# A decode block's last eight attention rounds in another order, products that fill TensorE's waits at the end, and another first inverse root

## The chip, the cores and the metric

The kernel runs on one core of one Trainium2 chip. A core has TensorE (PE, the matrix engine, with its weight loads shown as PEld), VectorE (DVE), ScalarE (ACT), GpSimd (POOL), SyncE (SP, which only issues transfers here) and 16 DMA engines. Each engine runs its own instructions strictly in the order in which the kernel wrote them, and waits on semaphores for the others. The metric is device time in microseconds (us) of one execution; lower is better.

## The reference

One decode step of a small transformer block in fp32: batch 4, model width 512, 32 query heads over 8 key/value heads, 4096 cached positions, head width 128, then a token-mixing MLP of width 1792.

```python
mod = (silu(c) @ w_mod).reshape(4, 6, 1, -1)          # sa, ca, ga, sb, cb, gb
h = layernorm(x) * (1 + ca) + sa
q = h @ wq
scores = q . k_cache * 128 ** -0.5                    # per batch and kv head
o = softmax(scores) @ v_cache
x = x + ga * (o @ wo)
h = layernorm(x) * (1 + cb) + sb
hn = layernorm(h)                                     # inside the mixer
u = gelu(hn * w1 + b1)                                # (batch, 512 channels, 1792)
x = x + gb * (u @ w2 + b2)
```

The caches are 128 MiB, the other weights some 22 MiB; nearly all of the work is to read them once.

## The kernel before

There are 32 rounds, one for each pair of batch (4) and key/value head (8); round i has a key tile K(i) and a value tile V(i) of 2 MiB each. A ring of three buffers of 4 MiB takes them: a load brings K(i+2) and V(i) together (line 192); near the end the loads come in smaller parts (lines 213 and 220), and the value tile of round 31 in four (32 position groups, cut at 16, 24 and 28). A load into a buffer waits until TensorE has used what was in it. All loads are issued by SP on one queue.

The steps of round i, as the table of the last eight rounds names them:

- `s` scores on TensorE (line 240), `S` row maximum on VectorE (245), `m` turn it (249), `X` maximum over the four column groups (254), `b` spread it to all partitions (260), `B` copy it (265), `e` exponential on ScalarE with a row sum (270).
- `t` transposes the two halves of the exponentials on VectorE (277); `l` sums over groups on TensorE (281), `L` their reciprocal and a selection matrix on VectorE (286, 292; in round 31 286, 289).
- `v` the product with the values on TensorE (303; in round 31 line 311, in four parts), `V` its copy out of PSUM (317), `a` picks and scales the heads (326), `A` copies (331), `p` multiplies by the output weights (339; in rounds 30 and 31 line 344, into one common accumulator `pgx`), `P` adds to the running sum of the batch (353, 355).

After a batch's eight rounds the mixer for it follows: fold (`F`, 360), residual and statistics (`R`, 364 to 374), two layer norms (`G`, `M`, `H`, `Q`, `N`), seven times an expansion `x` on VectorE (439, two of the 14 columns of w1 each), `g` gelu on ScalarE (495) and `c` the contraction with w2 on TensorE (444). Batches 0 to 2 run their mixers beside the next batch's rounds; batch 3's mixer comes at the end, after everything else. `f` (575) multiplies an eighth of the last two heads' output weights by the gate ga, so that rounds 30 and 31 need no gate at the end; `y` (360) folds rounds 24 to 29, `E` (364, 365) makes gate and residual of it, and `I` (693) adds that into `pgx` on TensorE.

For rounds 0 to 23 a loop writes the steps in a fixed order. For the last eight rounds the table `PLAN` is the order, written out by hand: the kernel walks through its words, and each word writes one step, so the table sets the order of instructions on every engine at once. `manual_schedule` leaves that order alone. `LP`, `LK`, `LV`, `LW` are loads and `LT` takes the next ring buffer; `T`, `T2`, `T3` load ScalarE's function tables early by a dummy call.

Batch 3's tail, the words from `zs` on, is a serial chain: statistics of `pgx` (`zs`), gather (`zq`, `zg`), the inverse root and the modulation (`zm`, `adaln_last`), spreading (`zb`), the second gather and norm (`zn`, `affine`), and `finish`: the 14 columns' gelus in seven groups, each followed by its contraction on TensorE, then the output. In `adaln_last` ScalarE makes a first value of the inverse root (407) and VectorE refines it by one step (409, 410) beside the difference from the mean (408); line 411 puts both together.

Of the kernel before, what the change touches and what calls it, by code (L numbers as in the profile page):

```python
# [8 lines left out]
F32 = mybir.dt.float32  # L9
I32 = mybir.dt.int32  # L10
AF = mybir.ActivationFunctionType
OP = mybir.AluOpType
# [21 lines left out]
def adaln_decode(ctx: ExitStack, tc: tile.TileContext, small, x, wmod, wq, kk, kv, vv, wo, out):  # L34
# [365 lines left out]

    def adaln_last(b, pst):
        mean, var = norm(pst)
        y = wk.tile([P, 1], F32, name="ye")
        t = wk.tile([P, 1], F32, name="te")
        a = wk.tile([P, P], F32, name="a")
        h1 = wk.tile([P, P], F32, name="h1")
        nc.scalar.activation(y, var, AF.Abs_reciprocal_sqrt, scale=1.0 / C2)
        dv.scalar_tensor_tensor(a, XK[:, b], mean, prep[:, 3], op0=OP.subtract, op1=OP.mult)
        dv.scalar_tensor_tensor(t, y, var, y, op0=OP.mult, op1=OP.mult)
        dv.scalar_tensor_tensor(y, t, 3.0 * C2, y, op0=OP.subtract, op1=OP.mult)  # L410
        dv.scalar_tensor_tensor(h1, a, y, prep[:, 2], op0=OP.mult, op1=OP.subtract)
        return h1, stats(h1, b)

    def bcast(h1, b, pb=None, cs=range(4)):
# [4 lines left out]
            mm(pb[:, c, :], ident[:, e:e + 1].to_broadcast([P, P]), h1, start=True, stop=True)  # L419
        return pb.rearrange("p c n -> p (c n)")  # L420

    def affine(pst, pb, times):
# [4 lines left out]
        if times is w1:  # L427
# [3 lines left out]
        if times is w1:  # L431
            nc.gpsimd.tensor_tensor(wr, w1, y.to_broadcast([P, NF]), op=OP.mult)
        else:
            rsqrt(var, P, "e", out=wr, times=times)
        return hb, wr

    def expand(u, hb, wr, js):
# [15 lines left out]
    class Mixer:  # L453
# [25 lines left out]
            self.pb = bcast(self.h1, self.b, pb, cs)  # L479

        def normalise(self):
            self.hb, self.wr = affine(self.st, self.pb, w1n if self.b < B - 1 else w1)
            self.py = None

        def expand(self, u=None):
# [53 lines left out]

    def finish(b, pg, py, hb, wr):  # L540
        uu = ring.tile([P, 16, D], F32, name="uu", tag="kv")
        for js in ((0,), (1,), (2, 3, 4), (5, 6, 7), (8, 9, 10), (11, 12), (13,)):
            j = js[0]
            if j < 2:
                nc.scalar.activation(uu[:, j], hb, AF.Gelu_apprx_tanh, bias=b1[:, j:j + 1], scale=wr[:, j:j + 1])
                u = uu[:, j:j + 1]
            else:
                u = uu[:, j:j + len(js)]
                expand(u, hb, wr, js)
                nc.scalar.activation(u, u, AF.Gelu_apprx_tanh)  # L550
# [8 lines left out]
        dv.scalar_tensor_tensor(osb[:, b], py, b2, gbl, op0=OP.add, op1=OP.mult)  # L559
        dv.tensor_add(osb[:, b], osb[:, b], XK[:, b])  # L560
        nc.sync.dma_start(dst[b], osb[8 * b:P:32, b])
# [75 lines left out]
    x LP27 m26 S27 f P24 m27 X26 X27 f b26 B26 e26 x b27 v25.1 c g t26.1 l25 t26.0 B27 s28 V25 c g L25  # L637
    v26.0 v26.1 S28 x l26 f a25 L26 V26 A25 x m28 p25 LT X28 e27 c a26 P25 t27.0 A26 b28 s29 f B28 p26 e28
    LK30 t27.1 S29 P26 v27.0 m29 l27 g LK31 T t28.1 X29 LT t28.0 s30 L27 S30 b29 v27.1 B29 e29 l28 m30 V27
    c LV28 L28 a27 g X30 t29.1 t29.0 l29 L29 s31 A27 LV29 b30 p27 x v28.0 B30 S31 m31 e30 f P27 LT LV30 X31  # L640
    v28.1 b31 l30 B31 e31 LV31 V28 L30 c t30.1 a28 l31 L31 v29.0 t31.1 v29.1 A28 p28 t30.0 V29 a29 v30.0
    A29 LW f v30.1 P28 p29 g V30 t31.0 a30 x v31.0 v31.1 v31.2 P29 A30 Y y f v31.3 p30 E V31 a31 I A31 p31
    zs g zq zg T2 c zx c zm zq zb0 zc T3 zg zb1 zw0 zn zw1
# [8 lines left out]
    for step in PLAN.split():  # L652
# [90 lines left out]
```

## Time and profile before

Each time is of one execution. The page's chain of waits is followed back from the last instruction; the lists of instructions in order of time give start and duration in us, engine, line, operation, written tile, read tiles, shapes, count, and in brackets how long the engine had been idle and whose work ended that.

| what | value |
|---|---|
| time, three runs | 389.9, 389.29, 389.33 us, median 389.33 |
| time of the profiled execution | 389.85 us |
| its span, first to last instruction | 387.7 us |
| mean clock granted to TensorE | 0.890 of full |
| moved by DMA | 157.70 MB, mean 407 GB/s |
| busy: PE, DVE, ACT | 297.5, 213.9, 107.9 us (77, 55, 28% of the span) |

Busy shares are means over the whole span. What counts for a change at the end is which wait ends last there.

### The profile page before, as it was taken

The numbers are of one execution on the slowest core, as the hardware profiler recorded it, in microseconds if no ns is written. First come the engines' busy times: TensorE is split into PE (matmuls) and PEld (weight loads), VectorE is DVE, ScalarE is ACT, GpSimd is POOL, SyncE is SP. The second block draws the span as 40 slices with busy tenths as digits, with TensorE's granted clock in tenths as the row PEclk, the third lists the DMA queues.
The fourth block names the chain that finished last, engine by engine and source line by source line (L and its number), as shares of the span: only waits on it lengthen the run. The fifth ranks groups of instructions, "written<-read, shape, count | busy, mean of one in ns | idle before, by whom it ended". The sixth has DMA issues, their size and how long they took to land.

```text
span 387.7 us, 5709 instructions
## 1 busy us (share of the span) xinstructions
PE 297.5 (77%) x2416; PEld 121.0 (31%) x2416; DVE 213.9 (55%) x510; ACT 107.9 (28%) x130; POOL 1.5 (0%) x8
## 2 busy tenths in 40 slices
PE   0776685962966829778788859999888886999984
PEld 0122121330322302234222323353323342445472
DVE  0420361530453605677666644767766678788666
ACT  0001120110110111114557110114782104657156
POOL 0000000000000000000000000000000000000000
PEclk9989666795596979999999995979999999799899
DMA  8999999999999999999999999999999999999900
GB/s 329 433 433 433 416 445 433 416 448 431 414 450 433 433 433 431 433 431 433 432 433 432 433 431 433 433 431 430 431 433 431 433 431 433 414 426 427 389 28 3
DMA packets 7281, 157.70 MB, mean 407 GB/s; under 512 B 964, under 2 KB 980, under 8 KB 1368
## 3 DMA queue, kind: packets, MB, share of 16 engines
q1 hardware_dynamic: 7248, 157.33, 94.6%
q8 instruction: 19, 0.31, 0.3%
q14 instruction: 6, 0.05, 0.0%
q10 hardware_dynamic: 8, 0.00, 0.0%
HBM read 157.32 MB, written 0.01 MB: 406 GB/s over the span
## 4 chain that ended last, share of the span: by engine, by line
DMA 43%; PE 36%; DVE 16%; ACT 3%; issue 1%; SPq 0%; ACTq 0%; DVEq 0%
DMA kv<-in_kv 41%; PE s L240 9%; PE pv L303 8%; DVE m L245 3%; PE pt L326 3%; PE pa L339 3%; DVE p L277 3%; PE s L139 2%; PE qs L154 2%; DMA sm<-in_small 2%; PE pb L260 2%; DVE mx L254 2%; ACT uu L550 1%; DVE acc L355 1%; PE py L444 1%
## 5 line engine op out<-in xcount | busy, mean ns | idle before, releaser
L240 PE MATMUL s<-kv,QT 128*32 128x512 f32 x512 | 75.4, 708 | 41.5 <-DMA kv<-in_kv 39.4
L270 ACT ACTIVATE p<-s,nm 128x1024 f32<-128x1024 f32 x32 | 35.6, 1114 | 196.2 <-DVE nm L265 196.1
L245 DVE TENSOR_REDUCE m<-s 128x1 f32<-128x1024 f32 x32 | 39.2, 1223 | 80.1 <-PE s L240 80.1
L303 PE MATMUL pv<-kv,p 128*32 128x512 f32 x496 | 75.0, 685 | 0.1
L277 DVE STREAM_TRANSPOSE p<-p 128x512 f32<-128x512 f32 x64 | 41.9, 687 | 1.7 <-ACT p L270 1.7
L240 PEld LDWEIGHTS s<-kv,QT 128*32 128x32 f32 x512 | 15.6, 121 | 85.6 <-DMA kv<-in_kv 53.9
L326 PEld LDWEIGHTS pt<-sel,po 128*128 128x128 f32 x250 | 33.1, 206 | 28.6 <-issue 17.5
L339 PE MATMUL pa<-wo,oT 128*32 128x512 f32 x240 | 35.0, 657 | 3.9 <-DVE oT L331 3.8
L326 PE MATMUL pt<-sel,po 128*128 128x4 f32 x250 | 35.7, 266 | 1.3 <-DVE po L317 1.3
L317 DVE COPY po<-pv 128x512 f32<-128x512 f32 x31 | 21.4, 689 | 17.2 <-PE pv L303 17.1
L254 DVE TENSOR_REDUCE mx<-pm 1x128 f32<-1x512 f32 x32 | 21.4, 671 | 0.7 <-PE pm L249 0.7
L495 ACT ACTIVATE u<-u 128x1024 f32<-128x1024 f32 x20 | 20.4, 1051 | 2.7 <-DVE u L439 2.6
L439 DVE TENSOR_SCALAR u<-hb,wr,sm 128x512 f32<-128x512 f32 x40 | 19.9, 540 | 1.0 <-PE py L450 0.9
L260 PEld LDWEIGHTS pb<-neg,mx 1*128 1x128 f32 x64 | 10.2, 198 | 32.6 <-DVE mx L254 30.9
L270 ACT ACT_TABLE_LOAD x11 | 14.1, 1283 | 20.5 <-DVE nm L265 20.4
L355 DVE TENSOR_TENSOR acc<-acc,pa 128x512 f32<-128x512 f32 x26 | 17.7, 681 | 2.4 <-PE pa L339 2.4
L139 PE MATMUL s<-wm,sT 128*4 128x512 f32 x16 | 9.7, 773 | 12.1 <-DVE sT L125 12.1
L303 PEld LDWEIGHTS pv<-kv,p 128*32 128x32 f32 x496 | 14.5, 147 | 8.0 <-issue 3.5
L260 PE MATMUL pb<-neg,mx 1*128 1x1 f32 x64 | 12.9, 268 | 5.0 <-DVE mx L254 5.0
L495 ACT ACT_TABLE_LOAD x13 | 16.7, 1283 | 0.2
L249 PE MATMUL pm<-ident,m 128*1 128x128 f32 x32 | 9.0, 283 | 9.7 <-DVE rl L286 4.0
L249 PEld LDWEIGHTS pm<-ident,m 128*1 128x1 f32 x32 | 2.5, 80 | 39.0 <-DVE rl L286 22.2
(146 smaller groups left out, 210.9 us busy)
## 6 DMA issues: line engine op xcount, KB each, us to landing
kv<-in_kv SPq DMA_DIRECT2D x28, 4096.0 KB, 21.3
wq<-in_wq SPq DMA_DIRECT2D x2, 4096.0 KB
wo<-in_wo SPq DMA_DIRECT2D x4, 2048.0 KB, 25.2
kv<-in_kv SPq DMA_DIRECT2D x4, 2048.0 KB, 17.6
wm<-in_wmod SPq DMA_DIRECT2D x2, 2048.0 KB, 7.9
kv<-in_kk SPq DMA_DIRECT2D x1, 4096.0 KB
kv<-in_vv SPq DMA_DIRECT2D x3, 1024.0 KB
wm<-in_wmod SPq DMA_DIRECT2D x1, 1024.0 KB
```

The costliest lines, as they stand in the source:

```text
L240: mm(s[32 * c:32 * c + 32, n * 512:(n + 1) * 512], QT[:, b, h, :], KT[i][:, (n * 4 + c) * 512:(n * 4 + c + 1) * 512], start=True, stop=True)
L245: dv.tensor_reduce(M[i], S[i], axis=AX.X, op=OP.max)
L254: dv.tensor_reduce(mx, M[i].rearrange("o (c r) -> o r c", c=4).unsqueeze(1).to_broadcast([1, 4, 32, 4]), axis=AX.X, op=OP.max)
L260: mm(pb, M[i].rearrange("o c r -> o (c r)"), neg1, start=True, stop=True)
L270: nc.scalar.activation(p, S[i], AF.Exp, bias=M.pop(i), accum_out=l)
L277: dv.transpose(p, p)
L303: mm(PV[i][32 * q:32 * q + 32, :], pT[:, 128 * k:128 * k + 128:4], VT[i][:, 4 * k:4 * k + 4, :].rearrange("p j d -> p (j d)"), start=(k < ...
L317: dv.tensor_copy(PV[i], pv)
L326: mm(pt, po[:, c * DH:(c + 1) * DH], sel[:, c, :], start=(c == 0), stop=(c == n - 1))
L339: mm(pa[32 * g:32 * g + 32, :], oT[:, g:g + 1].to_broadcast([P, 32]), wo_t[h][:, g, :], start=True, stop=True)
L355: dv.tensor_add(ACC[b], ACC[b], pa)
L495: nc.scalar.activation(u, u, AF.Gelu_apprx_tanh)
```

## The change

It has three parts.

First, the table `PLAN` is written in another order between round 23's `a` and round 31's `p`; the steps are the same, and from `zs` on the table is the same.

Second, in `finish` TensorE gets five more products after the contractions of columns 0, 1, 2 to 4, 5 to 7 and 8 to 10: the identity times 128 or 256 columns of a weight already in SBUF, into a PSUM tile `pad` that nobody reads.

Third, in `adaln_last` the inverse root is a reciprocal on VectorE and then a square root on ScalarE, with no refinement; the table that `T2` loads is the square root's. The sign of the modulated row is now the usual one, so `affine` uses the negated w1 for all batches.

```diff
     def adaln_last(b, pst):
         mean, var = norm(pst)
-        y = wk.tile([P, 1], F32, name="ye")
-        t = wk.tile([P, 1], F32, name="te")
+        q = wk.tile([P, 1], F32, name="qe")
+        r = wk.tile([P, 1], F32, name="ye")
         a = wk.tile([P, P], F32, name="a")
         h1 = wk.tile([P, P], F32, name="h1")
-        nc.scalar.activation(y, var, AF.Abs_reciprocal_sqrt, scale=1.0 / C2)
+        dv.reciprocal(q, var)
+        nc.scalar.activation(r, q, AF.Sqrt)
         dv.scalar_tensor_tensor(a, XK[:, b], mean, prep[:, 3], op0=OP.subtract, op1=OP.mult)
-        dv.scalar_tensor_tensor(t, y, var, y, op0=OP.mult, op1=OP.mult)
-        dv.scalar_tensor_tensor(y, t, 3.0 * C2, y, op0=OP.subtract, op1=OP.mult)
-        dv.scalar_tensor_tensor(h1, a, y, prep[:, 2], op0=OP.mult, op1=OP.subtract)
+        dv.scalar_tensor_tensor(h1, a, r, prep[:, 2], op0=OP.mult, op1=OP.add)
         return h1, stats(h1, b)
...
     def finish(b, pg, py, hb, wr):
         uu = ring.tile([P, 16, D], F32, name="uu", tag="kv")
+        pad = ps_e.tile([P, D], F32, name="pad", tag="e")
+        hold = {0: 128, 1: 256, 2: 256, 5: 256, 8: 256}
         for js in ((0,), (1,), (2, 3, 4), (5, 6, 7), (8, 9, 10), (11, 12), (13,)):
...
             contract(py, u, js)
+            if j in hold:
+                mm(pad[:, :hold[j]], ident, WM[5][:, 0, :hold[j]], start=True, stop=True)
...
     PLAN = """
-    a23 v24.0 A23 p23 t25.0 P23 F R v24.1 LP25 G s26 t25.1 M H V24 LP26 Q a24 S26 v25.0 N s27 x A24 f p24 g
...
+    LP25 t25.0 a23 A23 p23 P23 F v24.0 R v24.1 G s26 f M H Q t25.1 V24 LP26 a24 s27 N A24 S26 x v25.0
...
         elif step == "T2":
-            nc.scalar.activation(tab, neg1, AF.Abs_reciprocal_sqrt)
+            nc.scalar.activation(tab, ones[0:1, 0:1], AF.Sqrt)
```

What the new table does to the engines is seen in their instructions. The numbers behind the names count buffers; `x` is the two TENSOR_SCALAR that write `u`, `f` the TENSOR_TENSOR that writes `wo6`.

TensorE from round 31's scores (`s31`) to round 30's products with the values, before (`wo2` and `wo4` are output weights, `g32` and `grpl` are helpers for sums over groups):

```order
L240 MATMUL s31_2274<-kv_2146,QT_121 32x512 x8
L260 MATMUL pb_2286<-neg1_87,mx_2264 128x1
L339 MATMUL pa_2288<-wo2_126,oT_2283 32x512 x4
L303 MATMUL pv_2296<-kv_2211,p_2188 32x512 x4
L249 MATMUL pm_2305<-ident_99,m_2303 1x128
L303 MATMUL pv_2296<-kv_2211,p_2188 32x512 x4
L260 MATMUL pb_2321<-neg1_87,mx_2315 128x1
L281 MATMUL pl_2323<-l_2308,grp_117 128x1
L444 MATMUL py_2066<-u_2136,sm_88 32x128 x8
L326 MATMUL pt_2349<-sel_2256,po_2334 128x4 x4
L281 MATMUL pl_2354<-l_2328,grpl_119 128x1
L303 MATMUL pv_2360<-kv_2211,p_2236 32x512 x8
```

And of the change, at the same place:

```order
L240 MATMUL s31_2276<-kv_2080,QT_121 32x512 x8
L260 MATMUL pb_2286<-neg1_87,mx_2258 128x1
L339 MATMUL pa_2289<-wo2_126,oT_2268 32x512 x4
L303 MATMUL pv_2297<-kv_2220,p_2188 32x512 x4
L249 MATMUL pm_2306<-ident_99,m_2302 1x128
L303 MATMUL pv_2297<-kv_2220,p_2188 32x512 x4
L260 MATMUL pb_2319<-neg1_87,mx_2309 128x1
L443 MATMUL py_2047<-u_2148,sm_88 32x128 x8
L281 MATMUL pl_2339<-l_2316,grp_117 128x1
L326 MATMUL pt_2349<-sel_2255,po_2325 128x4 x4
L281 MATMUL pl_2354<-l_2343,grpl_119 128x1
L303 MATMUL pv_2361<-kv_2220,p_2238 32x512 x8
```

Only the contraction (`py`) and round 30's sum `l30` (`pl`) have changed places; from `v29` on, row by row, TensorE's order up to `finish` is the same in both kernels.

VectorE beside it, around round 31's row maximum `S31`, before:

```order
L439 TENSOR_SCALAR u_2293<-hb_1997,wr_1998,sm_88 128x512 x2
L265 COPY nm_2301<-pb_2286 128x1
L245 TENSOR_REDUCE m_2303<-s31_2274 128x1
L575 TENSOR_TENSOR wo6_128<-wo6_128,gate_1845 128x512
L355 TENSOR_TENSOR acc_2041<-acc_2041,pa_2288 128x512
L254 TENSOR_REDUCE mx_2315<-pm_2305 1x128
L265 COPY nm_2325<-pb_2321 128x1
L317 COPY po_2334<-pv_2296 128x512
```

And of the change:

```order
L438 TENSOR_SCALAR u_2294<-hb_2000,wr_2001,sm_88 128x512 x2
L245 TENSOR_REDUCE m_2302<-s31_2276 128x1
L265 COPY nm_2304<-pb_2286 128x1
L355 TENSOR_TENSOR acc_2043<-acc_2043,pa_2289 128x512
L254 TENSOR_REDUCE mx_2309<-pm_2306 1x128
L578 TENSOR_TENSOR wo6_128<-wo6_128,gate_1845 128x512
L265 COPY nm_2321<-pb_2319 128x1
L317 COPY po_2325<-pv_2297 128x512
```

`S31` now stands ahead of `B30` (the COPY that writes `nm` for round 30's exponential), and one `f` stands behind `X31` (line 254) where it stood ahead of `P27` (line 355).

VectorE from the last copy of a round's values to the modulation of the tail, before (line 317 with `pve` is `V31`):

```order
L331 COPY oT_2446<-pt_2409 128x4
L575 TENSOR_TENSOR wo6_128<-wo6_128,gate_1845 128x512
L364 TENSOR_TENSOR ep_2475<-pc_2449,prep_129 128x128
L365 TENSOR_TENSOR ep_2475<-ep_2475,prep_129 128x128
L317 COPY po_2478<-pve_2416 128x128
L331 COPY oT_2483<-pt_2480 128x4
```

And of the change:

```order
L331 COPY oT_2416<-pt_2409 128x4
L355 TENSOR_TENSOR acc_2043<-acc_2043,pa_2402 128x512
L317 COPY po_2474<-pve_2418 128x128
L364 TENSOR_TENSOR ep_2478<-pc_2449,prep_129 128x128
L365 TENSOR_TENSOR ep_2478<-ep_2478,prep_129 128x128
L331 COPY oT_2482<-pt_2476 128x4
L578 TENSOR_TENSOR wo6_128<-wo6_128,gate_1845 128x512
```

`V31` now stands ahead of `E` (lines 364, 365), and the last `f`, which was written ahead of `E`, now stands behind `A31` (the second COPY of `oT`), directly ahead of round 31's product with the output weights, whose last quarter reads what it writes.

More of the change, by code (lines that the diff above doesn't have):

```diff
@@ L420, in bcast, with affine @@
         return pb.rearrange("p c n -> p (c n)")
-    def affine(pst, pb, times):
+    def affine(pst, pb, last):
         mean, var = norm(pst)
@@ L425, in affine @@
         wr = wk.tile([P, NF], F32, name="wr")
-        if times is w1:
+        if last:
             y = wk.tile([P, 1], F32, name="ye")
@@ L430, in affine @@
         nc.scalar.activation(hb, pb, AF.Identity, bias=mean, scale=-1.0)
-        if times is w1:
-            nc.gpsimd.tensor_tensor(wr, w1, y.to_broadcast([P, NF]), op=OP.mult)
+        if last:
+            nc.gpsimd.tensor_tensor(wr, w1n, y.to_broadcast([P, NF]), op=OP.mult)
         else:
-            rsqrt(var, P, "e", out=wr, times=times)
+            rsqrt(var, P, "e", out=wr, times=w1n)
         return hb, wr
@@ L635, in adaln_decode @@
     PLAN = """
-    a23 v24.0 A23 p23 t25.0 P23 F R v24.1 LP25 G s26 t25.1 M H V24 LP26 Q a24 S26 v25.0 N s27 x A24 f p24 g
[L637 to L643, printed above, removed]
+    LP25 t25.0 a23 A23 p23 P23 F v24.0 R v24.1 G s26 f M H Q t25.1 V24 LP26 a24 s27 N A24 S26 x v25.0
+    LP27 S27 f m26 p24 X26 g x P24 m27 c f b26 X27 v25.1 B26 b27 l25 e26 x t26.0 g t26.1 LT x B27 s28
+    V25 v26.0 S28 c g l26 L25 v26.1 a25 f L26 c V26 A25 e27 x m28 p25 X28 P25 a26 t27.0 A26 b28 s29 f
+    B28 v27.0 e28 LK30 p26 t27.1 S29 P26 m29 l27 s30 X29 g LK31 T t28.1 LT t28.0 S30 b29 L27 v27.1 B29
+    V27 e29 l28 m30 c L28 LV28 X30 a27 g t29.1 t29.0 A27 l29 L29 s31 LV29 b30 LT p27 x v28.0 S31 B30 m31
+    P27 X31 v28.1 e30 f b31 B31 LV30 V28 c LV31 l30 t30.1 e31 L30 a28 l31 t31.1 L31 v29.0 v29.1 A28 LW
+    p28 t30.0 g V29 a29 v30.0 t31.0 v30.1 A29 f P28 p29 V30 a30 x A30 v31.0 v31.1 v31.2 Y P29 y v31.3
+    p30 V31 a31 E I A31 f p31 zs g zq zg T2 c zx c zm zq zb0 zc T3 zg zb1 zw0 zn zw1
     """
```

2 lines of the change are left out of this document (1 added, 1 removed).

## The prediction

> **What bounds the kernel now.** I read the page's slices first, then the transfers' issues, then TensorE in order of time from round 31 on, then the clock by stretches of the gate's own length, and last the tail.
>
> ```profile
> span 387.7 us, 5709 instructions
> PEclk9989666795596979999999995979999999799899
> DMA  8999999999999999999999999999999999999900
> ```
>
> A slice is 9.69 us. The DMA engines are full from the start to slice 38, whatever the compute engines do. Then come two slices of tail. So a step of the table matters only if it makes a transfer land later, or if it lies behind the last landing.
>
> ```profile
> 350.39 0.43 SPq L220 DMA_DIRECT2D kv<-in_vv  x1
> kv<-in_vv SPq DMA_DIRECT2D x1, 256.0 KB, 17.5
> ...
> 353.26 0.22 PEld L303 LDWEIGHTS pv<-kv,p 128*32 128x32 f32 x8 [0.73 <-DMA kv<-in_kv]
> ```
>
> The last piece of round 31's values lands at 350.39 + 17.5 = 367.9. It was issued 17 us ahead, so a release that comes several us later or earlier leaves the landing where it is. And at 353.26 TensorE had been idle for 0.73 us for round 28's values: whatever was lost or won in rounds 24 to 30 was made up there, with 0.73 us to spare.
>
> ```profile
> 354.49 1.09 PE L303 MATMUL pv<-kv,p 128*32 128x512 f32 x8
> 356.24 0.64 PE L444 MATMUL py<-u,sm 128*32 128x128 f32 x16
> 356.84 1.05 PE L326 MATMUL pt<-sel,po 128*128 128x4 f32 x8
> 357.75 0.36 PE L281 MATMUL pl<-l,grpl 128*128 128x1 f32 x2
> 358.21 3.20 PE L303 MATMUL pv<-kv,p 128*32 128x512 f32 x16
> 361.11 1.61 PE L339 MATMUL pa<-wo,oT 128*32 128x512 f32 x8
> 363.63 1.95 PE L303 MATMUL pv<-kv,p 128*32 128x512 f32 x16
> 365.40 1.04 PE L339 MATMUL pa<-wo,oT 128*32 128x512 f32 x8
> ```
>
> Round 29's values are 2048 KB behind round 28's. At the 431 GB/s of the row below (351.95) that is 2.10 MB / 431 = 4.9 us, so they land at about 353.2 + 4.9 = 358.1: `v29`, at 358.21, sits on its landing too. It took 3.20 us where `v30`, of the same shape, took 1.95, and `p28` 1.61 where `p29` took 1.04. That is 1.25 + 0.57 = 1.8 us lost to the clock:
>
> ```profile
> 351.95:355.37 3.42, 3.42 (x31) 0.96 (x27) 3.19 (x6) 2.49 (x3) 0.00 (x0) 1.00 1.01 431
> 355.37:358.78 3.41, 3.29 (x42) 2.52 (x42) 2.46 (x9) 2.48 (x3) 0.00 (x0) 1.00 0.97 411
> 358.78:362.19 3.41, 3.41 (x24) 0.88 (x16) 1.77 (x4) 1.07 (x2) 0.00 (x0) 0.50 1.01 418
> 379.26:382.67 3.41, 1.73 (x50) 1.20 (x50) 3.41 (x8) 3.41 (x4) 0.00 (x0) 1.00 0.00 0
> 382.67:386.09 3.42, 1.80 (x48) 1.12 (x48) 1.65 (x5) 1.41 (x2) 0.00 (x0) 1.00 0.03 7
> ```
>
> Columns: stretch, its length, busy us of PE, PEld, DVE, ACT, POOL, granted clock, DMA share, GB/s. The clock was halved for 3.41 us behind a stretch in which PE counts as busy for 3.29 us, but mostly with small products: four columns (356.84) or one (357.75). So the sparse stretch that costs something is the one between `v28`'s second half (354.49) and `v29`.
>
> **The change, part by part.** The sum is made against the profiled execution, 389.85 us (span 387.7 and 2.15 around it). The median of the runs, 389.33, is 0.52 lower, so I carry the difference over to the median.
>
> *Rounds 24 to 30.* The same steps stand in another order; no transfer is added and SP's order stays. A gain here ends at 353.26, since `v28` waits for its landing: 0. A loss is free up to 0.73 us and beyond that moves `v28` and `v29` one for one. A load's cover, at the last piece, is 17.5 us less the 0.6 us that 256 KB need at 431 GB/s; a release would have to come more than ten us late to leave the queue empty. I take 0.
>
> *Round 31's `S31` ahead of `B30`.* TensorE's order is the same there but for one exchange, so what decides is VectorE.
>
> ```profile
> 352.56 1.21 DVE L245 TENSOR_REDUCE m<-s 128x1 f32<-128x1024 f32 x1
> 352.72 1.28 ACT L270 ACT_TABLE_LOAD   x1 [0.97 <-DVE nm L265]
> 354.02 1.11 ACT L270 ACTIVATE p<-s,nm 128x1024 f32<-128x1024 f32 x1
> 356.28 1.11 ACT L270 ACTIVATE p<-s,nm 128x1024 f32<-128x1024 f32 x1 [1.06 <-DVE nm L265]
> ```
>
> `B30` was at 352.5 and now follows `S31`, at about 353.6. ScalarE then loads the table until 355.1, does `e30` until 356.2 and its sum until 356.3, and `e31` until about 357.5 instead of 357.4: the 1.06 us for which ScalarE waited ahead of `e31` take the delay up. `l31` (357.75) comes behind `a28`, which ends at 357.9. So `v29` moves by 0 to 0.1: +0.05. The cover is gone as soon as `S31` itself is late, which is the slower rival.
>
> *From `v29` to round 31.* TensorE's order is unchanged, and so is the sparse stretch ahead of it. I therefore keep the halved clock: 0.
>
> ```profile
> 368.43 0.68 DVE L575 TENSOR_TENSOR wo<-wo,gate 128x512 f32<-128x512 f32 x1
> 369.15 0.40 PE L311 MATMUL pve<-kv,p 128*32 128x128 f32 x8
> 369.37 1.06 PE L344 MATMUL pgx<-wo,oT 128*32 128x128 f32 x32
> 369.94 0.28 DVE L317 COPY po<-pve 128x128 f32<-128x128 f32 x1
> 370.36 0.30 PEld L326 LDWEIGHTS pt<-sel,po 128*128 128x128 f32 x2 [0.20 <-DVE po L317]
> 371.00 1.08 PE L344 MATMUL pgx<-wo,oT 128*32 128x128 f32 x32
> ```
>
> *`V31` ahead of `E`.* `V31` ran at 369.94, 0.4 us after round 31's last values (369.15 + 0.40), because `E` stood ahead. `a31` waited 0.20 us for it; now that wait goes, but `p30` holds TensorE until 370.43. Bounds 0 and -0.20; I take -0.1. `E` ends later, at about 370.5, just as `I` needs it. The last `f` (0.68 us) now starts with `p31` behind `A31`; it must be done for `p31`'s last quarter, which begins three quarters of 1.08 us = 0.81 later. Bounds 0 and +0.1, taken into the range.
>
> *The inverse root.*
>
> ```profile
> 350.89 0.12 DVE L286 RECIPROCAL rl<-pl 128x1 f32<-128x1 f32 x1
> 373.46 0.35 DVE L408 SCALAR_TENSOR_TENSOR a<-xk,mv,prep 128x128 f32<-128x128 f32 x1
> 373.46 0.20 ACT L407 ACTIVATE ye<-mv 128x1 f32<-128x1 f32 x1 [3.00 <-DVE mv L389]
> 374.18 0.35 DVE L411 SCALAR_TENSOR_TENSOR h<-a,ye,prep 128x128 f32<-128x128 f32 x1
> ```
>
> Before, 374.18 - 373.46 = 0.72 us lie between statistics and modulation. Now: reciprocal 0.12 to 0.17, then `a` 0.35 on VectorE, beside it ScalarE's square root, priced as line 407's 0.20, each with a hand-over below 0.1. That makes 0.50 to 0.55: -0.2 (bounds -0.25 and -0.1). One table is loaded in place of another; the gelu's table then loads 0.2 later, under the wait for `hb`.
>
> *The five filling products.*
>
> ```profile
> 375.38 0.69 PE L419 MATMUL py<-h,ident 128*128 128x128 f32 x4
> 382.66 1.89 PE L444 MATMUL py<-uu,sm 128*32 128x128 f32 x48 [0.51 <-ACT uu L550]
> 383.61 0.68 PEld L444 LDWEIGHTS py<-uu,sm 128*32 128x32 f32 x24 [0.35 <-ACT uu L550]
> 384.62 0.35 DVE L559 SCALAR_TENSOR_TENSOR osb<-py,sm,gbl 128x128 f32<-128x128 f32 x1 [0.92 <-PE py L444]
> ```
>
> Two products of the identity with 128 columns took 0.69 (375.38), so one of 256 takes at most that, and about 0.5 when only its columns count. The first four lie in waits for ScalarE. The fifth does not: behind columns 8 to 10 (begun 382.66) TensorE waited only 0.35 us, until 383.61. The fill pushes the last contractions by 0.15 to 0.34, and 0.1 of that is won back ahead of column 13. Bounds 0 and +0.45; I take +0.15.
>
> Sum: 0.05 - 0.1 - 0.2 + 0.15 = -0.1 us, 389.2 on the median. With the bounds of these terms alone, and half a us of wander as between the runs shown, the case spans 388.6 to 389.9.
>
> The fills are there for the clock. In the Trainium skill, "TensorE: Matmul & The Clock Gate", section "HAM oscillation — how this bites in real kernels", the rule of thumb is that no idle gap of TensorE may exceed about 3.4 us. By that rule the tail, whose waits are far shorter, keeps its clock anyway and the fills only cost: the same -0.1. The trace does not bear the rule out as it stands: the clock fell at 358.78 behind a stretch with 0.12 us idle.
>
> **The rivals.** *Faster: the clock falls differently.* The tail's stretches in rows 379.26 and 382.67 have 1.7 to 1.8 us of short products and kept the clock in this trace. The stretch from 355.37 lost it; there only `v28`'s end (0.2 us), one contraction (0.64) and `v29`'s start (0.6) stream many columns, about 1.4 us in all. So the tail is near the edge. If stretches fall 1 us later, one holds only the first columns' contractions, and the last ones run at half speed. Columns 8 to 13 took 1.89 us with their waits; at half speed the products would need up to 1.7 us more, of which the waits for ScalarE hide a part. I estimate a cost of 0.9 to 1.3 us in such runs of the kernel before, which the fills take away: 389.3 - 0.9 - 0.1 = 388.3. Or the halved clock at `v29` is missed: round 31's last products then follow their landing at 367.9 instead of 369.15, -1.25, also about 388.2. Against it: one trace, with the tail at 1.00. The Trainium skill, same page, section "What's actually happening", states that the window of 3413 ns is free-running and does not reset with the kernel; the stretches of 3.41 us agree, but only several traces could show that they shift between executions.
>
> *Slower: VectorE late at `S31`.* It was busy for 3.19 of the 3.42 us from 351.95, and the new table has other steps ahead of `S31`. If `S31` begins 1 us later than 352.5, `e30`'s table load, `e30` and `e31` follow, `l31` holds TensorE, and `v29` starts at about 359.2; with the clock halved it all arrives 0.9 later: 389.2 + 0.9 = 390.1 to 390.3. It decides from about 0.2 us of lateness on. Against it: the 0.73 us of slack at `v28`, and VectorE's work ahead of this place is the same steps.
>
> *No effect at all on the path* is within the first case, since three of its four terms are 0.2 or less.
>
> **Chances.** A measurement of this kernel can tell about 0.2%, 0.8 us, from no change. The first case, 389.2, has 0.50; the faster one (below 388.55) 0.33; the slower one (above 390.1) 0.17. The range reaches into both: 388.0 to 390.2.
>
> **What would show it.** `v28` again waits for its transfer at about 353.2 and `v29` starts at 358.2; `v29` takes about 3.2 us if the clock falls again, 1.9 if not. The wait of `a31` for `V31` is gone. From the second-last statistics to `h` there are about 0.5 us. The last contraction starts behind the fifth fill, not behind ScalarE. Wrong would be: `v28` without a wait, a gap in the DMA share before 366, or a clock of 1.00 from 355 to 366.

## The result and the profile after

The changed kernel takes 391.59 us (median of 6 runs, 390.36 to 392.05), the kernel before 389.30 in the 6 runs beside it (388.78 to 389.90): a ratio of 1.0053 with a 95% interval of 1.0033 to 1.0074. It is slower by about 2 us, where 389.2 was predicted. (A ratio given here is worked out from the runs and is not the quotient of the two medians.)

The profiled execution is the changed kernel's fastest, 390.36 us. Its page again first:

```profile
span 388.2 us, 5728 instructions
PEclk9998555975695975989999985978999989899999
DMA  8999999999999999999999999999999999999900
```

The DMA engines are as full as before. In the clock's row slice 33 (310 to 320 us) now reads 8 where it was 9, and slice 38 (359 to 369 us) 9 where it was 8, and other slices differ too: the clock falls at other places. TensorE from the end of round 23's values on, and the same stretch by pieces of 3.41 us (length, busy us of PE, PEld, DVE, ACT, POOL, granted clock, DMA share, GB/s):

```profile
306.68 1.10 PE L303 MATMUL pv<-kv,p 128*32 128x512 f32 x8
308.59 1.05 PE L326 MATMUL pt<-sel,po 128*128 128x4 f32 x8 [0.81 <-DVE po L317]
309.90 1.06 PE L339 MATMUL pa<-wo,oT 128*32 128x512 f32 x8 [0.25 <-DVE oT L331]
311.78 0.63 PE L360 MATMUL pc<-acc,g 128*32 128x128 f32 x8 [0.81 <-DVE acc L355]
312.17 3.44 PE L303 MATMUL pv<-kv,p 128*32 128x512 f32 x16
316.20 1.92 PE L240 MATMUL s<-kv,QT 128*32 128x512 f32 x16
```

```profile
308.49:311.90 3.41, 2.24 (x20) 1.25 (x24) 1.51 (x4) 0.00 (x0) 0.00 (x0) 0.99 0.96 408
311.90:315.31 3.41, 3.41 (x24) 0.88 (x20) 1.66 (x5) 0.00 (x0) 0.00 (x0) 0.51 0.96 413
```

And the kernel before at this place:

```profile
308.44 1.05 PE L326 MATMUL pt<-sel,po 128*128 128x4 f32 x8 [0.81 <-DVE po L317]
309.48 1.10 PE L303 MATMUL pv<-kv,p 128*32 128x512 f32 x8
310.36 1.07 PE L339 MATMUL pa<-wo,oT 128*32 128x512 f32 x8
312.48 1.04 PE L303 MATMUL pv<-kv,p 128*32 128x512 f32 x8
314.27 1.92 PE L240 MATMUL s<-kv,QT 128*32 128x512 f32 x16
```

```profile
308.49:311.90 3.41, 2.94 (x24) 1.49 (x24) 1.19 (x3) 0.00 (x0) 0.00 (x0) 1.00 0.93 404
```

Before, `v24`'s first half (309.48) filled the wait between `a23` and `p23`. Now the whole of `v24` stands behind the fold, and from 307.8 to 312.2 TensorE has one product with 512 columns, `p23`, between three waits (0.81, 0.25 and 0.81 us). At 311.90 the clock halves, `v24` takes 3.44 us where its halves took 1.10 + 1.04, and `s26` is 1.93 us late (316.20 against 314.27).

By `s29` 0.64 us of this is made up (1.29 us late, 341.92 against 340.63; `s28` takes 2.82 us where it took 3.64 before), and by `s31` 0.84 is lost again (2.13 late, 352.34 against 350.21). TensorE's and VectorE's rows on the way, in order of time:

```profile
331.44 2.82 PE L240 MATMUL s<-kv,QT 128*32 128x512 f32 x16 [1.82 <-ACT p L270]
346.38 0.38 PE L281 MATMUL pl<-l,grp 128*128 128x1 f32 x2 [0.61 <-DVE acc L355]
346.69 1.92 PE L240 MATMUL s<-kv,QT 128*32 128x512 f32 x16
352.34 1.92 PE L240 MATMUL s<-kv,QT 128*32 128x512 f32 x16
355.39 1.04 PE L303 MATMUL pv<-kv,p 128*32 128x512 f32 x8
360.02 1.95 PE L303 MATMUL pv<-kv,p 128*32 128x512 f32 x16
363.77 1.95 PE L303 MATMUL pv<-kv,p 128*32 128x512 f32 x16
369.29 0.40 PE L311 MATMUL pve<-kv,p 128*32 128x128 f32 x8
```

```profile
345.63 0.69 DVE L355 TENSOR_TENSOR acc<-acc,pa 128x512 f32<-128x512 f32 x1 [0.49 <-PE pa L339]
348.68 1.23 DVE L245 TENSOR_REDUCE m<-s 128x1 f32<-128x1024 f32 x1 [0.56 <-PE s L240]
```

`p26` now stands behind `v27`'s first half, so `P26` on VectorE (345.63) waits 0.49 us for it; `l27` on TensorE (346.38) waits 0.61 us for `P26`, and `s30` comes behind it. At `v28` (355.39) TensorE no longer waits for the transfer: it is 2.12 us behind 353.27. `v29` starts 1.81 us late but at full clock, and `v30` and round 31's last values stand 0.14 us behind those of before. So in this execution the order's loss is hidden by a halved clock that the other profile has at `v29`.

The tail: the inverse root, the fifth filling product with the last contractions, and the output row.

```profile
373.60 0.16 DVE L407 RECIPROCAL qe<-mv 128x1 f32<-128x1 f32 x1
374.13 0.35 DVE L410 SCALAR_TENSOR_TENSOR h<-a,ye,prep 128x128 f32<-128x128 f32 x1
383.50 0.70 PE L554 MATMUL pad<-kv,ident 128*128 128x256 f32 x2
384.13 0.86 PE L443 MATMUL py<-uu,sm 128*32 128x128 f32 x24
385.06 0.35 DVE L562 SCALAR_TENSOR_TENSOR osb<-py,sm,gbl 128x128 f32<-128x128 f32 x1 [1.40 <-PE py L443]
```

From the statistics to `h` it is 374.13 - 373.60 = 0.53 us, 0.72 before: -0.19. From the second norm's output on, the output row comes 0.48 us later than before (8.22 us behind VectorE's first `uu`, at 376.84; before 384.62 - 376.88 = 7.74). Sum of this execution: 0.14 - 0.19 + 0.48 = +0.43; measured 390.36 - 389.85 = +0.51.

### The profile page after: what moved, and what is told of

The parts are those of the page before. It is cut to its first block, busy times and chain, and to the rows that moved or that the text cites. A ratio compares the mean times of both kernels' runs of the same rounds, so it can differ in the third digit from the quotient of the medians.

```text
span 388.2 us, 5728 instructions
## 1 busy us (share of the span) xinstructions
PE 304.6 (78%) x2426; PEld 124.6 (32%) x2426; DVE 214.3 (55%) x509; ACT 107.9 (28%) x130; POOL 1.5 (0%) x8
## 4 chain that ended last, share of the span: by engine, by line
DMA 48%; PE 34%; DVE 15%; ACT 2%; issue 1%; SPq 1%; ACTq 0%
DMA kv<-in_kv 41%; PE s L240 9%; PE pv L303 8%; DMA wq<-in_wq 6%; DVE m L245 3%; PE pt L326 3%; DVE p L277 3%; PE pa L339 3%; PE py L443 2%; DVE mx L254 2%; PE pb L260 1%; DVE acc L355 1%; PE qs L154 1%; PE pl L281 1%; PE phb L418 1%
## 5 line engine op out<-in xcount | busy, mean ns | idle before, releaser
L240 PE MATMUL s<-kv,QT 128*32 128x512 f32 x512 | 78.2, 732 | 36.2 <-DMA kv<-in_kv 31.5
L303 PE MATMUL pv<-kv,p 128*32 128x512 f32 x496 | 75.9, 693 | 0.2 <-DVE po L317 0.2
L139 PE MATMUL s<-wm,sT 128*4 128x512 f32 x16 | 8.5, 694 | 11.8 <-DVE sT L125 11.8
```

The costliest lines, as they stand in the source:

```text
L240: mm(s[32 * c:32 * c + 32, n * 512:(n + 1) * 512], QT[:, b, h, :], KT[i][:, (n * 4 + c) * 512:(n * 4 + c + 1) * 512], start=True, stop=True)
L303: mm(PV[i][32 * q:32 * q + 32, :], pT[:, 128 * k:128 * k + 128:4], VT[i][:, 4 * k:4 * k + 4, :].rearrange("p j d -> p (j d)"), start=(k < ...
```

## The experiments

Each kernel ran 12 times (`plan_hold` 9, `fill_four` 11) beside 32 to 35 runs of the kernel before, whose median was 389.15 to 389.35 each time. One program's times spread over some 3 us: of the kernel before's 142 runs 135 lie between 388.33 and 390.15 us and the other seven between 391.28 and 391.78, with none between. A median moves when such groups' shares move. So the traces are read beside the medians: of each, the start of some steps, in us (o: the old table's words, n: the new table's; the middle is `s26` to `s29`, the end from `s29` on). In the code cuts of this section a line of the table can end ahead of its last word.

| kernel | start, middle, end | s26 | s28 (its length) | s29 | s31 | v28 | v29 (its length) | median |
|---|---|---|---|---|---|---|---|---|
| before | o o o | 314.27 | 329.73 (3.64) | 340.63 | 350.21 | 353.27 | 358.21 (3.20) | 389.15 to 389.35 |
| old_late | n o o | 317.03 | 332.78 (1.95) | 341.50 | 351.09 | 354.13 | 358.92 (1.95) | 389.15 |
| old_then_new | o o n | 314.36 | 329.85 (2.32) | 338.85 | 349.27 | 353.32 | 358.26 (1.95) | 389.12 |
| late_old_new | n o n | 317.34 | 333.08 (2.04) | 341.81 | 352.23 | 355.27 | 359.90 (1.95) | 389.88 |
| new_then_old | n n o | 315.58 | 330.83 (3.64) | 341.32 | 350.91 | 353.95 | 358.74 (1.95) | 390.01 |
| plan_v24 | o n n | 316.37 | 331.63 (3.64) | 342.96 | 353.38 | 356.42 | 361.05 (1.95) | 389.40 |
| plan_only | n n n | 317.10 | 332.34 (3.64) | 342.91 | 353.33 | 356.38 | 361.01 (1.95) | 390.96 |
| plan_hold | n, filled; n n | 314.55 | 329.79 (3.64) | 341.01 | 351.43 | 354.47 | 359.10 (1.95) | 389.81 |
| after | n n n | 316.20 | 331.44 (2.82) | 341.92 | 352.34 | 355.39 | 360.02 (1.95) | 391.59 |
| after_hold | n, filled; n n | 314.69 | 329.93 (3.33) | 339.92 | 350.34 | 353.38 | 358.19 (1.95) | 388.98 |
| after_mended | n, filled; n, p26 back | 314.61 | 329.86 (3.22) | 339.74 | 349.58 | 353.32 | 358.27 (1.95) | 388.58 |

### One part of the change at a time

`plan_only` is the kernel before with the new table, `fill_only` with the five filling products, `root_only` with the new inverse root. `plan_v24` is `plan_only` with the first words as they were, so that `v24` is back in its place (`LP25` and `t25.0` go back with it):

```diff
-    LP25 t25.0 a23 A23 p23 P23 F v24.0 R v24.1 G s26 f M H Q t25.1 V24 LP26 a24 s27 N A24 S26 x v25.0
+    a23 v24.0 A23 p23 t25.0 P23 F R v24.1 LP25 G s26 f M H Q t25.1 V24 LP26 a24 s27 N A24 S26 x v25.0
```

> The kernel before with the new table alone; the five filling products and the new inverse root are left out. Three theories. Table: the loss is the new order's, so this kernel keeps nearly all of it; fills cost 0.4 us and the root gives 0.2, so 391.6 - 0.4 + 0.2 = 391.4, ratio about 1.005, and v29 starts at 360, not 358.2. Fills: they cost most of the 2.3 us; then this kernel stays within 0.5 us of the kernel before, ratio 1.000 to 1.001. Chance: the changed kernel only met worse stretches of the clock; then this one scatters between 389 and 391 with no clear ratio.

> The kernel before with the five filling products alone; the table and the inverse root are the old ones. By the trace of the changed kernel the fifth product moves the last contractions by 0.4 to 0.5 us: 389.7, ratio 1.001, if the clock of the tail is full anyway. If the tail's clock is often halved in the kernel before, the products win that back: 388.5 to 389.0, ratio 0.998 to 0.999. If the fills are the cause of the loss: 391, ratio 1.004.

> The kernel before with reciprocal and square root in place of the refined inverse root alone. From statistics to modulation 0.53 us instead of 0.72, as in the trace of the changed kernel, so 389.1, ratio 0.9995, by every theory; above 389.5 the table load or the hand-over to ScalarE would cost something that the trace does not show.

> The new table, with its first words put back as they were, so that round 24's products with the values stand again before and between round 23's last steps and not behind them; no fills, old root. Theory sparse start: the new table opens a stretch of 4 us with few columns on TensorE at 308 to 312, the clock halves there and round 26's scores start 1.9 us late, which VectorE never makes up; with the words back s26 starts at 314.3 and the time is that of the kernel before, 389.3 within 0.4, ratio 0.999 to 1.001. Theory VectorE's order: S26 behind the second norm, and four expansions ahead of B27, make round 28 late by themselves; then s26 is at 314.3 but s28 stays about 1 us or more late and the ratio stays at 1.003 or more.

Measured: `plan_only` 390.96, ratio 1.0028 (1.0010 to 1.0046); `fill_only` 390.15, 1.0009 (0.9992 to 1.0025); `root_only` 388.77, 0.9987 (0.9973 to 1.0001); `plan_v24` 389.40, 1.0007 (0.9989 to 1.0025). The table is what costs, and by the medians most of it goes with the first words, though the two intervals overlap and four of `plan_v24`'s twelve runs stand at 391.0 to 391.2. The profile of one of those has the halved clock at the start too; the first half of `v24`, put back:

```profile
309.91 1.95 PE L303 MATMUL pv<-kv,p 128*32 128x512 f32 x8
```

So putting `v24` back makes the fall rarer, not impossible. Over the profiles of all experiments, the clock halves at the start in two of the seven with the old first words (`plan_v24`, and `fill_four`, where `s26` comes at 315.90), and in all seven with `v24` behind the fold and no products added. `fill_only`'s profile kept the clock at `v29`, and shows the tail's cost (the output row waits 1.40 us for TensorE there too):

```profile
357.99 1.95 PE L303 MATMUL pv<-kv,p 128*32 128x512 f32 x16 [0.17 <-DMA kv<-in_kv]
383.66 0.35 DVE L563 SCALAR_TENSOR_TENSOR osb<-py,sm,gbl 128x128 f32<-128x128 f32 x1 [1.40 <-PE py L444]
```

With `v29` at full clock `pve`'s last piece came at 367.69, before at 369.15: the halved clock there is worth 1.46 us, if it falls there. The fills still lose 0.48 us from `uu` to the output row (383.66 - 375.44 = 8.22), and its median is 0.45 above the 389.7 that was expected.

### Is it the sparse start, and is it the clock?

`old_late` makes the sparse start alone, in the old table: only `v24`'s first half moves. `plan_hold` keeps the whole new table, and lets TensorE multiply the identity in the start's waits (word `h`, 256, 128 and 256 columns), into a PSUM tile that nobody reads:

```diff
-    a23 v24.0 A23 p23 t25.0 P23 F R v24.1 LP25 G s26
+    a23 A23 p23 t25.0 P23 F v24.0 R v24.1 LP25 G s26
```

```diff
-    LP25 t25.0 a23 A23 p23 P23 F v24.0 R v24.1 G s26
+    LP25 t25.0 h256 a23 h128 A23 p23 h256 P23 F v24.0 R v24.1 G s26
...
+        elif op == "h":
+            pad = ps_e.tile([P, D], F32, name="pad", tag="e")
+            mm(pad[:, :i], ident, gate[:, :i], start=True, stop=True)
```

> The order of the kernel before, with one change: round 24's first half (v24) stands behind round 23's product and the fold, as in the new table. Theory (the sparse start costs it): from the end of v23 at about 307.6 to the fold at about 312 TensorE has no dense product but p23; the clock is halved there in nearly every execution, s26 comes 1.5 to 3 us later than 314.27, v28 no longer waits for its transfer, median 390.5 to 391.0. Rival (the rest of the new order, rounds 25 to 31, costs it): 389.1 to 389.4, v28 waits at 353.2.

> The whole new table, old inverse root, no fills in the tail, but three products of the identity with 256, 128 and 256 columns around a23 and p23, in the waits between v23 and v24. Theory (it is the clock of the start): the clock stays at 1.00 from 306 to 318, s26 at 314.3 to 315.0 though TensorE has up to 1.75 us more to do, median 389.0 to 389.5. Rival 1 (the order of VectorE's steps costs it, the clock is a side effect): as the new table alone, about 390.9. Rival 2 (the new order from round 25 on gains once the start is mended): below 388.7.

Measured: `old_late` 389.15, ratio 1.0003 (0.9985 to 1.0021); `plan_hold` 389.81, 1.0011 (0.9993 to 1.0029). The theory that the start alone costs the time falls with `old_late`: the clock does halve there, for 6.8 us, and `s26` is 2.76 us late, yet at `v28` 0.86 is left:

```profile
317.03 1.93 PE L240 MATMUL s<-kv,QT 128*32 128x512 f32 x16
332.78 1.95 PE L240 MATMUL s<-kv,QT 128*32 128x512 f32 x16
354.13 1.04 PE L303 MATMUL pv<-kv,p 128*32 128x512 f32 x8
```

By the table the old middle makes it up at `s28`: behind the late start the next halved stretch (before: 6.8 us from 328.1) lasts from 329.5 to 332.9 only and ends as `s28` begins (332.78), which takes 1.95 us and not 3.64. Where the halved piece falls differs between executions, so this is how this execution made it up, not a property of the old middle that is shown. In the new table `s28` takes 2.4 to 3.6 us in every profile, and in `plan_hold`, whose start is good, the time from `s29` to `s31` is 10.42 where the old table has 9.58. `plan_hold`'s median is above the 389.0 to 389.5 that its theory gave. So a second theory: there are losses in the middle and at the end, too, and together with the start's they are more than is made up ahead of `v28`.

### The table in pieces

The two tables hold the same steps up to `s29`, so they can be joined there. `new_then_old` is the new table up to `s29` and the old from there; `old_then_new` the other way round; `late_old_new` is `old_late` up to `s29` and the new table from there. The end's first words, old and new:

```diff
-    s29 f B28 p26 e28 LK30 t27.1 S29 P26 v27.0 m29 l27 g LK31 T t28.1 X29 LT t28.0 s30
+    s29 f B28 v27.0 e28 LK30 p26 t27.1 S29 P26 m29 l27 s30 X29 g LK31 T t28.1 LT t28.0
```

> The new table up to round 29's scores (s29), from there on the table of before; old inverse root, no fills. Theory (two losses add up: the sparse start, which makes s26 2 to 3 us late, and the exchange of p26 and v27.0 behind s29, by which VectorE waits 0.5 us for p26 and s30 and s31 come 0.83 us later): from s29 to s31 it takes 9.6 us and not 10.4, v28 starts 0.8 us earlier than with the whole new table, median 389.9 to 390.4, against 390.96. Rival 1 (the new end costs it all): 389.2. Rival 2 (the new order between s26 and s29 costs it, the end does not matter): 390.9.

> The table of before up to s29, from there on the new table; old inverse root, no fills. Theory of two losses: from s29 to s31 10.4 us, v28 no longer waits for its transfer and starts at 353.3 to 354.1, which is at most 0.2 us beyond the slack; median 389.2 to 389.6. Rival 1 (the new end costs it all): 390.5 to 391. Rival 2 (the new order between s26 and s29): 389.2, as before.

> The table of before with v24 behind the fold (the sparse start), and from s29 on the new table; between them the old order. Theory of two losses: alone, the late start was worth nothing (389.15) since the old order takes most of it up, and the new end uses up what slack is left: v28 at 354.9 to 355.3, v29 at 359.6 or later, median 389.8 to 390.4. Rival 2 (the middle, s26 to s29, is what keeps the start's loss from being taken up): 389.2 to 389.5.

Measured: `new_then_old` 390.01, ratio 1.0030 (1.0004 to 1.0056); `old_then_new` 389.12, 0.9996 (0.9980 to 1.0011); `late_old_new` 389.88, 1.0013 (0.9995 to 1.0030). From `s29` to `s31` every profile with the whole new end takes 10.42 us and those with the old end 9.58 or 9.59 (but for `root_hold` below, where `s30` waits 0.58 us for its transfer). In the medians the new end is worth nothing behind the good start (389.12) and 0.7 behind the sparse one (389.15 to 389.88); the new middle is worth 0.9 there (389.15 to 390.01); both together 1.8 (390.96). So by the medians the losses of the three parts add behind the sparse start. The intervals are as wide as the steps, and `new_then_old` and `late_old_new` have six runs below and six above a gap in which their medians lie, so the 0.7 and the 0.9 are rough; it is the traces that carry the end's 0.84. With the good start `old_then_new` still waits for its transfer: from `s31` to `v28` it takes 4.05 us, and 3.04 in `old_late`, where `v28` does not wait. That is so because its middle took 24.49 us, where the profile of before took 26.36 with the clock halved for the whole of `s28`.

### In the changed kernel itself

Four edits of the changed kernel: `after_hold` is the start's three products alone; `after_p26` puts `p26` ahead of `v27` again; `after_four` leaves the fifth filling product out; `after_mended` does all three.

```diff
-    B28 v27.0 e28 LK30 p26 t27.1 S29 P26 m29 l27 s30
+    B28 p26 e28 LK30 v27.0 t27.1 S29 P26 m29 l27 s30
...
-        hold = {0: 128, 1: 256, 2: 256, 5: 256, 8: 256}
+        hold = {0: 128, 1: 256, 2: 256, 5: 256}
```

> The changed kernel with three products of the identity (256, 128, 256 columns) in the waits of its sparse start, and nothing else. Theory (the clock of the start): no halved clock between 306 and 318, s26 at 314.3 to 314.8, median 1 to 1.5 us below the changed kernel, 390.0 to 390.6. Rival (the steps' order alone, so that s26 comes as late again): 391.5.

> The changed kernel with one exchange undone: round 26's product with the output weights (p26) stands again ahead of round 27's first half with the values (v27.0). Theory (this exchange alone makes VectorE wait 0.5 us for p26, and l27 and s30 wait for VectorE): from s29 to s30 4.2 us and not 4.76, from s29 to s31 9.8 to 9.9 and not 10.4, v28 about 0.6 us earlier, median 390.8 to 391.2. Rival (another move between s29 and s31 costs it): 10.4, 391.5.

> The changed kernel without the fifth filling product. Theory (the fifth lies on the path, the other four do not): the last contraction no longer starts behind a product, 0.4 to 0.5 us saved behind the second norm, median 391.0 to 391.2. Rival (without it the clock falls in the last contractions and they take it all back): 391.5.

> All three: the start's products, p26 ahead again, no fifth fill. Theory (three losses that together are the change's loss, with the root's gain left): v28 waits for its transfer again, median 388.5 to 389.0, below the kernel before. Rival (a fourth loss, between s26 and s29 or behind v29): 389.5 or more.

Measured: `after_hold` 388.98, ratio 0.9999 (0.9984 to 1.0014); `after_p26` 390.76, 1.0035 (1.0017 to 1.0053); `after_four` 390.05, 1.0022 (1.0004 to 1.0041); `after_mended` 388.58, 0.9988 (0.9973 to 1.0003). The start's three products are the experiment that decides: nothing else is changed, TensorE has 1.87 us more to do, and the kernel is 2.6 us faster than the changed one, with intervals that lie apart. The gain is larger than the 1 to 1.5 us that were expected. The start of `after_hold`, by the same pieces, and the steps behind it:

```profile
308.49:311.90 3.41, 3.01 (x21) 1.64 (x20) 1.60 (x4) 0.00 (x0) 0.00 (x0) 1.00 0.94 399
311.90:315.31 3.41, 3.35 (x36) 1.67 (x40) 2.14 (x8) 0.00 (x0) 0.00 (x0) 1.00 0.98 423
```

```profile
307.80 0.70 PE L688 MATMUL pad<-gate,ident 128*128 128x256 f32 x2
309.59 0.47 PE L688 MATMUL pad<-gate,ident 128*128 128x128 f32 x2
310.99 0.70 PE L688 MATMUL pad<-gate,ident 128*128 128x256 f32 x2
312.18 1.92 PE L303 MATMUL pv<-kv,p 128*32 128x512 f32 x16
314.69 1.92 PE L240 MATMUL s<-kv,QT 128*32 128x512 f32 x16
353.38 1.04 PE L303 MATMUL pv<-kv,p 128*32 128x512 f32 x8
358.19 1.95 PE L303 MATMUL pv<-kv,p 128*32 128x512 f32 x16
```

The clock stays at 1.00, `v24` takes 1.92 us and not 3.44, and `v28` comes at 353.38, 0.11 us later than before. Eleven of its twelve runs lie within 388.73 to 389.36, closer together than those of any other kernel here.

`after_p26` shows its exchange as priced: from `s29` to `s30` 4.18 us and not 4.77.

```profile
343.85 1.92 PE L240 MATMUL s<-kv,QT 128*32 128x512 f32 x16
348.03 1.92 PE L240 MATMUL s<-kv,QT 128*32 128x512 f32 x16
353.69 1.92 PE L240 MATMUL s<-kv,QT 128*32 128x512 f32 x16
```

To `s31` it is 9.84, so 0.58 of the end's 0.84 us is this exchange, and 0.26 lies between `s30` and `s31`, in another move that was not tried alone. This profile (391.62 us) and that of `after_four` (391.26) also show what most executions of the changed kernel are likely to look like (four of its six runs stand at 391.5 to 392.05), which its own profile, taken of its fastest run, does not: at the start the clock is halved there for 10.2 and 6.8 us, `v28` comes at 356.73 and 356.76, and round 31's last values at 370.64 and 370.67, 1.4 us behind the profiled execution's 369.29 and 2.8 behind `after_hold`'s 367.88. That is about what `after_hold` gains in the median. `after_four` lies 1.5 us below the changed kernel and 1 below what was expected, where the fifth product is worth 0.48 in the traces; six runs on the one side and times in groups are a likely reason, but that was not settled.

In `after_mended` `v28` waits for its transfer again, as before the change:

```profile
353.32 1.09 PE L303 MATMUL pv<-kv,p 128*32 128x512 f32 x8 [0.52 <-DMA kv<-in_kv]
```

It keeps the new middle, which therefore costs nothing that its median shows once the start is filled.

### Fills and root without the new table

`fill_four` is the kernel before with four fills; `root_four` has the new root as well; `root_hold` is `root_only` with products of the identity in two sparse stretches:

```diff
-    a23 v24.0 A23 p23 t25.0 P23 F R v24.1
+    h256 a23 v24.0 A23 p23 t25.0 h128 P23 F R v24.1
...
-    v28.1 b31 l30 B31 e31 LV31 V28 L30 c t30.1 a28 l31 L31 v29.0
+    v28.1 h128 b31 l30 B31 e31 LV31 V28 L30 c h128 t30.1 a28 l31 L31 v29.0
```

> The kernel before with the first four filling products and without the fifth (behind columns 8 to 10). Theory (only the fifth lies on the path): median 389.2, 0.4 to 0.9 below all five (390.15), and the last contraction starts behind ScalarE's gelu again. Rival (all of them cost, each a little): 389.8 to 390.2.

> The table of before, with the new inverse root and the first four filling products, without the fifth. Theory: the root's 0.2 to 0.3 us come on top of the tail with four fills: most runs at 388.2 to 388.5, median 388.4. Rival (the fills only moved the phase of the clock's stretches in those runs): 388.8, as the root alone.

> The kernel before with the new inverse root, and with products of the identity in two sparse stretches: 256 and 128 columns around round 23's product, and 128 columns twice between v28 and v29. Theory (the clock halved at v29 is worth 1.25 to 1.45 us in those executions that have it): v29 takes 1.95 us in every execution, all times between 388.0 and 388.8, median 388.3 to 388.5, against 388.77 for the new root alone. Rival (the products push l31 and v29 by as much as the clock gives, or the halved clock turns up a stretch later): 388.8 to 389.3.

Measured: `fill_four` 388.68, ratio 0.9992 (0.9974 to 1.0010); `root_four` 388.69, 1.0002 (0.9981 to 1.0022); `root_hold` 388.90, 0.9986 (0.9976 to 0.9996). In `fill_four` the output row waits as long for TensorE as in the kernel before:

```profile
383.46 0.35 DVE L563 SCALAR_TENSOR_TENSOR osb<-py,sm,gbl 128x128 f32<-128x128 f32 x1 [0.92 <-PE py L444]
```

It comes 383.46 - 375.72 = 7.74 us behind `uu`, with five fills 8.22: the fifth is the whole cost and the other four are free. (Its `s26` was 1.6 us late, behind a halved clock at the start, and the time is 388.68 all the same.) `root_four` is not faster than `fill_four` in the median, so the root's 0.2 us could not be seen on top; three of its runs stand at 391.1 to 391.3, and no profile caught what happens in those. In `root_hold`'s profile `v29` takes 1.95 us, but it starts at 358.44, 0.23 us later than before, and the median is no lower than with the root alone (388.77): the rival's number. Its mechanism is not shown, since this execution, at 388.39, is one of the fastest; no profile caught the runs at 389.1 to 390.35. No version is shown to beat the kernel before by more than 0.2%; the lowest median is `after_mended`'s 388.58.

## Why the prediction was wrong

*Rounds 24 to 30: "A loss is free up to 0.73 us", "I take 0".* This is the step that failed, in its slack and in its size. The condition was stated (a loss beyond the slack at `v28` moves `v28` and `v29` one for one), but the 0.73 us are idle time of the weight loads (PEld, up to 353.26) and not of the products: `p27`'s ran meanwhile, from 352.38 for 1.07 us. `s28`, `s31`, `p27` and `v28` before:

```profile
329.73 3.64 PE L240 MATMUL s<-kv,QT 128*32 128x512 f32 x16 [0.74 <-ACT p L270]
350.21 1.92 PE L240 MATMUL s<-kv,QT 128*32 128x512 f32 x16
352.38 1.07 PE L339 MATMUL pa<-wo,oT 128*32 128x512 f32 x8
353.27 1.10 PE L303 MATMUL pv<-kv,p 128*32 128x512 f32 x8
```

And `p27` in `old_late`, where `v28` waits for no transfer and starts at 354.13:

```profile
353.25 1.06 PE L339 MATMUL pa<-wo,oT 128*32 128x512 f32 x8
```

`v28` starts 0.89 us behind the start of `p27` before and 0.88 in `old_late`; from `s31` it is 3.06 and 3.04. So in the profiled execution the products had 0.02 us to spare, and a delay at `s31` passes whole to `v28`: 0.88 becomes 0.86 in `old_late`, 2.13 becomes 2.12 in the changed kernel. Where the middle runs faster there is some slack (1.0 us in `old_then_new`, whose `s28` took 2.32 us and not 3.64).

The size was put at nothing without a look at the order ahead of `s31`. It measured 2.12 us at `v28` in the changed kernel's fastest execution, and 3.5 in the profiles of its two variants without good starts. Two sources are shown: the sparse start, whose halved clock makes `s26` 1.9 to 2.8 us late (by `after_hold`), and the end, 0.84 us, of which the exchange of `p26` and `v27` is 0.58 and another move 0.26 (by the joined tables and `after_p26`). The middle is the third part, and its share stays open. `s28` waits 1.0 to 1.8 us for ScalarE there, but it does not come late by that: it starts 15.24 us behind `s26` in the changed kernel, 15.46 before and 15.75 in `old_late`. What can cost is the clock: `s28` takes 2.4 to 3.6 us in all nine profiles with the new middle, and 1.9 to 3.6 in the nine with the old one. Against the profile of before, which has it too, the new middle gains the 0.64 us above: 1.93 - 0.64 + 0.84 = 2.13. Behind a late start it loses 1.3 (24.47 us in `old_late`, 25.81 in `plan_only`). Its moves were not taken apart.

*`S31` ahead of `B30`, +0.05.* From `s31` to `v29` it is 7.68 us (352.34 to 360.02), and in the old table 7.83 where `v28` and `v29` wait for no transfer (`old_late`, 351.09 to 358.92). So the new order there costs nothing and is 0.15 us shorter, all its moves together. The slower rival put the lateness at `S31` itself. `S31` did start 1.77 us late (354.33 against 352.56), but because `s31` was 2.13 late. Its price was too small: it had `v29` at 359.2 and 390.1 to 390.3, and the measured median is 391.59.

*From `v29` on, the halved clock kept: 0.* Wrong in the profiled execution: `v29` starts later, a different piece of 3.41 us holds the sparse stretch, and `v29` takes 1.95 us. The faster rival said that this could be missed, at 1.25 us; `fill_only` shows 1.46. It came true, and hid most of the order's loss in that one execution, which is luck of the execution that was profiled: the profile before, against which the sum was made, is one of only two of the 18 that have `v29` at half clock. Two of the prediction's own signs of being wrong came with it, `v28` without a wait and a clock of 1.00 from 355 to 366.

*`V31` ahead of `E`, -0.1.* Nothing. `V31` runs 0.18 us earlier, but `a31`'s weights are loaded 0.99 us behind the start of `p30` in both kernels, which points to `p30` and not to `V31`, and the wait ahead of `a31` is still 0.20:

```profile
370.50 0.30 PEld L326 LDWEIGHTS pt<-sel,po 128*128 128x128 f32 x2 [0.20 <-DVE ep L364]
```

*The inverse root, -0.2.* Right: 0.53 us for 0.72. Alone, it gave a ratio of 0.9987, whose interval just touches 1.

*The five fills, +0.15.* The mechanism was right (four hidden, the fifth not), the size was not: +0.48, just beyond the upper bound of 0.45. Nothing is won back ahead of the last column: the fifth product of 256 columns takes 0.70 us, where about 0.5 was taken as possible. What the fills were worth for the tail's clock did not show: `plan_only`'s last contractions ran at half clock from about 381 to 384, and its output row still came 385.75 - 378.01 = 7.74 us behind `uu`.

## What to carry to other kernels

Where a hand-written order changes, read from the trace, at every place where a many-column product is moved, what TensorE has left in the 3.4 us around it; a product that fills a wait can be worth more than its own time, and a few products of the identity in the waits can take its place. Before a wait for a transfer is taken as slack, read whose wait it is: 0.73 us of the weight loads were 0.02 us of the products. And what slack there is belongs to the whole stretch ahead of it, and differs between executions. And where times of one program stand in groups, one profile can hide the loss: compare the profiles of several near kernels before a term is set to zero.

## What the hardware did that was not expected

In the changed kernel a granted clock of one half followed a stretch (308.49 to 311.90) in which no wait of TensorE was longer than 0.81 us. The Trainium skill, "TensorE: Matmul & The Clock Gate", section "HAM oscillation — how this bites in real kernels", gives as a rule of thumb that gaps must stay below about 3.4 us; here the trace differs: the gap was 0.81 us and the clock fell to 0.51. Nor does counted busy time decide. In the kernel before the clock fell behind a piece with 3.29 busy us of 3.41 (355.37) and stayed up behind one with 1.73 (379.26). Most of the first one's busy time is of products of four columns or one, which suggests that what counts is how many columns are streamed; no run varied the columns alone. With 1.87 us of products added in that stretch, in the same waits, the clock stayed up in the profiled executions of all three kernels that had them (`plan_hold`, `after_hold`, `after_mended`).

The prediction left open whether the pieces of 3.41 us shift between executions. They do: `s26` starts at 314.27, 314.27 and 314.35 in the profiles of the kernel before, `root_only` and `fill_only`, whose order is the same up to there and beyond, and the next halved piece begins at 328.05, 327.85 and 325.96.

How much a halved piece costs depends on what lies in it: 1.46 us at `v29`, nothing at the end of `plan_only`, and at `s28` about 1.7 us (3.64 against 1.95 in `old_late`, whose piece ended as `s28` began).
